# Another written order and another choice of engines for a recurrent attention with a Fourier mix and an FFN

## The chip, the core and the metric

The kernel runs on one core of a Trainium2 chip. The metric is the device time of one execution in microseconds (us). The core has TensorE (PE, matrix products; its weight loads are listed as PEld), VectorE (DVE), ScalarE (ACT), GpSimd (POOL) and SyncE (SP, which issues transfers). Each engine works through its own queue in order; an instruction that waits holds up all that stand behind it on that engine.

## What is computed

Four batches of 768 rows; eight heads of 64 make 512 columns. First a linear recurrence with one decay for each head, then the real part of a two-dimensional Fourier transform added to its input, a normalisation of each row, and an FFN of width 2048 with a residual:

```python
for t in range(S):
    state = gamma[None, :, None, None] * state + einsum('bhd,bhe->bhde', k[:, :, t], v[:, :, t])
    y[:, :, t] = scale * einsum('bhd,bhde->bhe', q[:, :, t], state)
...
x = y.transpose(0, 2, 1, 3).reshape(B, S, H * D)
u = x + real(fft(fft(x, axis=1), axis=2))
un = (u - mean(u)) / sqrt(var(u) + 1e-06)
out = u + relu(un @ w_ch1) @ w_ch2
```

## The kernel before

The recurrence is done in chunks of 128 rows. Heads go in pairs, so there are four pairs (the last number of a piece's name, 0 to 3) and six chunks. For each pair the queries, keys and values are loaded (`lq`, `lk`, `lv`, by SP), cast to 16 bit (`q`, `k`, `v` in batch 0, `cq`, `ck`, `cv` in the later ones) and transposed on PE through PSUM (`tq`, `tk`), from where an engine copies them (`eq`, `ek`). In batch 0 the keys are transposed back (`kb`, copy `eb`). PE forms the products of queries and keys (`am`, later `a`, L574 and L694), DVE masks them (`ae`, L583; later `m`, L705), PE forms the states (`kv`), DVE runs them through the decay (`sc`, a scan, L607; later `s1` to `s4`, L731), PE forms the output from state and masked product (`yx`, `yi`, later `y`), and an engine scales its rows (`x`). The Fourier transform over the rows folds the rows first (`fs`, `fl`, `fh`, `fd`, `fe` on DVE, L785 to L811), multiplies with cosine and sine tables (`s1..`, then copies `g`, `gr`), and does the columns by a second product (`s2`), whose halves are combined into u by DVE (`u0`, `u1`, after a copy `q0`, `q1`) and the input added (`ux`, by POOL or DVE). `g0a`, `g0b`, `g0c` are a small edge column. Statistics of the rows (`bn` on DVE, `rt` on ACT, `rc`, `nb`) give the normalised rows (`un`), which are transposed (`ut`, `te`). In the FFN `h` is the first product with the weights and `r` its relu; the second one adds its 2048 terms in the order of a fast matrix product: sums of halves of relu results (`hs`, on DVE, L1300) go into products (`m1a` to `m7b`, L1329) and sums of those into u (`w`, L1374).

Batch 0 is also the start. While its first loads run, the tables of cosines and sines are made on the chip: steps 0 to 4 of `ta` (product, L403), `tn` (rounded copy), `tb` (product, L406) and `ab`, `co`, `si` on ACT. Batches 1, 2 and 3 follow, and the FFN of one batch is mixed with the attention of the next.

What sets the order: every piece of work is a function in a dictionary, and the table ORDER lists all their names. `play` (L1591) calls them one after another, and `pin` (L232) ties the instructions of each engine into that order. So ORDER is an order for all five queues at once, and only the place of a piece among the pieces of its own engine counts, beside its data. Buffers are taken in this order as well: products of PE go to five PSUM buffers of one group, to two of another and, after the start, to three of a third, and a product waits until the buffer's last reader is done.

A second table, ENGINES, names the engine of each piece that more than one can do: A, D or P for ACT, DVE, POOL. The helpers `copied` (L260) and `scaled` (L265) take that letter and issue the copy or the scaling there; a relu, an addition of x and a few more read it in their own pieces.

The piece `f512` is `filler(512)` (L257, L258): a product of 128x128 with 128x512 zeros into a PSUM buffer that nobody reads. It is given 16 times in ORDER; eight more are issued before ORDER begins.

Loads of batch 1 wait for two things: a load of weights (`w22`) and the matmul `h13` of the first FFN half of batch 0. Loads of later batches wait for a product of the batch before.

Of the kernel before, what the change touches and what calls it, by code (L numbers as in the profile page):

```python
# [18 lines left out]
P = 128  # L19
B, H, S, D = 4, 8, 768, 64  # L20
# [22 lines left out]
h12:A qn4:A h13:A xu2:D h03:A un2:A h11:A h01:A te2:A xl4:P xu4:P xu3:P xl0:D un3:A xu0:D h10:A
h20:D un4:A h21:A qn5:D xl5:P 1ck1_0:P te3:A h22:A 1cq_0:D 1ck0_0:D 1ek_0:D 1eq0_0:A 1eq1_0:A
xu5:P 1cv_0:P 1s0_0:A un5:A 1cq_1:A te4:D 1ck0_2:A 1ck0_1:P 1ck1_1:P mp7:P 1eq1_1:A 1eq0_1:A
1cv_1:P 1ek_1:A 1x1_0:A mp3:P 1x0_0:A h23:A 1cv_2:P 1ck1_2:A 1s0_1:D te5:A 1cq_3:P 1cq_2:A
1ck0_3:P 1s0_2:D 1cv_3:P 1ek_2:A mp4:P 1eq1_2:A 1ck1_3:P 1eq0_2:A 0r1_12:A 1eq1_3:A 1eq0_3:A
1x1_1:A 1x0_1:A 1s0_3:A 0r1_5:A 1ek_3:A 0r1_7:A 0r1_8:A 1x0_2:A 1x1_2:A 2cv_1:A 2cq1_1:A
# [47 lines left out]
0h1_12 2cq1_1 1kv1_2 1m2_2 1a0_3 0r1_6 2lk2 0r1_12 mp4 1s3_2 0h1_11 0r1_11 1s4_2 1m0_3 1a2_3 1m2_3
# [1532 lines left out]
```

## Time and profile before

| | |
|---|---|
| median of three runs | 235.96 us (235.61 to 236.78) |
| profiled execution | 236.86 us |
| its span, first to last instruction | 234.9 us |
| busy: PE, DVE, ACT, POOL | 228.9, 203.4, 144.3, 91.3 us |
| granted clock | 1.0 |
| bytes: read, written | 27.26, 6.29 MB |

A row of the profile's timeline has the start in us, the duration, the engine, the line of the kernel, the operation, the tiles as out<-in, the shapes and a count of like instructions that were put together; in brackets stands the idle time of the engine before it and what ended it. A row of grouped instructions has instead the busy time in us, the mean duration of one in ns, and the idle time ahead of the group with what ended it. Instructions of one engine that follow directly on each other overlap a little in the records.

### The profile page before, as it was taken

How to read it: one execution, taken by the hardware profiler on the slowest of the kernel's cores; microseconds unless marked ns; L12 is line 12 of the kernel's file. 1: busy time of each engine (PE TensorE's matmuls, PEld its weight loads, DVE VectorE, ACT ScalarE, POOL GpSimd, SP SyncE). 2: the span in 40 equal slices, each digit the busy share in tenths (PEclk: the TensorE clock that was granted, in tenths of full speed). 3: DMA queues.
4: the chain of work that ended last, by engine and by line, in shares of the span. 5: the costliest groups of instructions: out<-in, count | busy, mean ns of one | idle time of the engine just before them, and what ended most of it. 6: DMA issues, size and time to landing. Idle time of an engine off the chain costs nothing.

```text
span 234.9 us, 6332 instructions
## 1 busy us (share of the span) xinstructions
PE 228.9 (97%) x2471; PEld 187.1 (80%) x2471; DVE 203.4 (87%) x527; ACT 144.3 (61%) x303; POOL 91.3 (39%) x144
## 2 busy tenths in 40 slices
PE   7999999999999999999999999999999999999994
PEld 2566888856776855889999989888898988888884
DVE  6599989966899999999999999999988698875494
ACT  7599786688998856671976493565644615241220
POOL 4789133452440378226315707404007161330302
PEclk9999999999999999999999999999999999999999
DMA  7999997999999999999969956632700224130034
GB/s 199 311 290 178 207 166 116 257 228 247 220 213 201 211 209 176 198 195 182 237 161 202 201 129 126 156 77 81 237 3 4 45 89 114 22 47 0 4 125 143
DMA packets 94253, 36.45 MB, mean 155 GB/s; under 512 B 83600, under 2 KB 91408, under 8 KB 94224
## 3 DMA queue, kind: packets, MB, share of 16 engines
q1 hardware_dynamic: 89856, 31.79, 63.9%
q0 software_dynamic: 4224, 4.19, 11.5%
q8 instruction: 19, 0.31, 0.6%
q14 instruction: 10, 0.08, 0.1%
q10 hardware_dynamic: 144, 0.07, 0.1%
HBM read 27.26 MB, written 6.29 MB: 143 GB/s over the span
## 4 chain that ended last, share of the span: by engine, by line
PE 73%; ACT 1%; DVE 0%; issue 0%
PE psh L1267 27%; PE psc L1329 24%; PE psc L1223 6%; PE psh L1183 4%; PE wkA L694 3%; PE ps L840 3%; PE pq L1024 2%; PE wkY L753 2%; PE wkY L744 1%; PE wkK L717 1%; ACT qTz L262 1%; PE tq L669 1%; PE psh L1205 0%; PE pst L1167 0%; PE ps L974 0%; ACT x L267 0%
## 5 line engine op out<-in xcount | busy, mean ns | idle before, releaser
L1267 PE MATMUL psh<-unT,w 128*128 128x256 f16 x576 | 67.7, 273 | 0.0
L1267 PEld LDWEIGHTS <-w 128*128 128x128 f16 x576 | 55.8, 98 | 6.6 <-DVE u L1374 0.2
L1276 ACT ACTIVATE ht<-psh 128x512 f16<-128x512 f32 x65 | 37.4, 596 | 30.5 <-PE psh L1267 22.7
L1329 PEld LDWEIGHTS <-ht 128*128 128x128 f16 x360 | 34.1, 98 | 4.2 <-DVE ht L1300 0.3
L1329 PE MATMUL psc<-w,ht 128*128 128x256 f16 x192 | 26.2, 272 | 0.0
L705 DVE TENSOR_TENSOR atm<-wkA,maskp 128x512 f16<-128x512 f32 x36 | 23.9, 682 | 1.5 <-PE wkA L694 1.5
L1060 POOL TENSOR_TENSOR u<-u,x 128x256 f32<-128x256 f32 x31 | 19.7, 654 | 14.2 <-DVE u L1050 7.9
L1223 PE MATMUL psc<-w,ht 128*128 128x512 f16 x96 | 23.3, 379 | 0.0
L1374 DVE TENSOR_TENSOR u<-psc,u 128x256 f32<-128x256 f32 x42 | 16.7, 416 | 6.6 <-PE psc L1329 5.8
L1374 POOL TENSOR_TENSOR u<-u,cd 128x512 f32<-128x512 f32 (+1 forms) x8 | 8.9, 1119 | 27.9 <-DVE cd L1374 27.9
L267 ACT ACTIVATE x<-wkY,gexp 128x384 f16<-128x384 f32 x29 | 16.1, 583 | 5.6 <-PE wkY L753 4.1
L731 DVE SCALAR_TENSOR_TENSOR s<-s,gk,wkK 128x128 f16<-128x128 f16 x48 | 16.1, 341 | 2.2 <-ACT s L262 1.5
L1118 DVE BATCH_NORM_STATS2 bst<-u 128x6 f32<-128x512 f32 x24 | 16.3, 681 | 0.2
L263 POOL COPY g16r<-g 128x384 f16<-128x384 f16 x6 | 3.4, 579 | 31.5 <-ACT g L262 19.0
L1223 PEld LDWEIGHTS <-ht 128*128 128x128 f16 x96 | 8.7, 98 | 7.7
L262 ACT COPY qn<-pq 128x127 f32<-128x127 f32 (+2 forms) x31 | 7.9, 299 | 11.0 <-PE pq L1024 5.1
L1374 POOL TENSOR_TENSOR u<-u,ws 128x256 f32<-128x256 f32 (+1 forms) x6 | 5.7, 978 | 20.5 <-DVE ws L1374 20.5
L1399 ACT ACTIVATE un<-u,stats 128x512 f16<-128x512 f32 x12 | 9.5, 812 | 5.8 <-DVE stats L1392 5.8
L694 PE MATMUL wkA<-qTz,kT 128*128 128x256 f16 x72 | 12.4, 272 | 0.3 <-ACT unT L262 0.2
L268 POOL TENSOR_SCALAR kd<-k,gexp 128x384 f16<-128x384 f32 x15 | 9.4, 629 | 6.8 <-DMA k<-in_k_dram 4.8
L1183 PE MATMUL psh<-unT,w 128*128 128x384 f16 x64 | 11.9, 326 | 0.0
L1205 PE MATMUL psh<-unT,w 128*128 128x128 f16 x192 | 11.7, 219 | 0.0
(238 smaller groups left out, 508.5 us busy)
## 6 DMA issues: line engine op xcount, KB each, us to landing
q<-in_q_dram SPq DMA_DIRECT2D x16, 384.0 KB, 6.2
k<-in_k_dram SPq DMA_DIRECT2D x16, 384.0 KB, 5.6
v<-in_v_dram SPq DMA_DIRECT2D x16, 384.0 KB, 6.3
w<-in_moe_w_ch_dram POOLq DMA_DIRECT2D x8, 512.0 KB, 7.8
out_dram<-u SPq DMA_DIRECT2D x6, 512.0 KB, 3.4
out_dram<-u SPq DMA_DIRECT2D x6, 256.0 KB, 3.9
out_dram<-o SPq DMA_DIRECT2D x2, 512.0 KB, 3.2
out_dram<-o SPq DMA_DIRECT2D x3, 128.0 KB, 1.8
```

Source lines behind the costliest of these rows:

```text
L267: return nc.scalar.activation(out, in_, AF.Copy, bias=0.0, scale=scale)
L694: mm = nc.tensor.matmul(wk[:, c2], st["kT"][:, c, :], st["qT"][:, :, c, :], start=True, stop=True)
L705: nc.vector.tensor_tensor(out=st["atm"][:, 2 * part:2 * part + 2], in0=st["wk", part], in1=maskp[:, PAIR_ORDER[i]].unsqueeze(1).to_broadca ...
L731: nc.vector.scalar_tensor_tensor(out=s16[:, c], in0=s16[:, c - 1], scalar=gk2[:, hp:hp + 1], in1=st["kv", c // 3][:, c % 3], op0=ALU.mult, ...
L1060: (nc.vector if on.get(f"{b}ux{n}_{kb}", "P") == "D" else nc.gpsimd).tensor_tensor(out=u[:, lo:hi], in0=u[:, lo:hi], in1=x[:, 1, 257:1:-1] ...
L1118: nc.vector.bn_stats(bst, lb[b]["u"][:, kb, :])
L1183: nc.tensor.matmul(psh, w116[:, cb, fb * P:(fb + 1) * P], lb[b]["unT"][:, cb, rt * 384:(rt + 1) * 384], start=(cb == 0), stop=(cb == 3))
L1223: nc.tensor.matmul(lb[b]["psc", rb], ht16[:, fb, rb % 3 * P:rb % 3 * P + P], w216[:, fb, :], start=(fb == 0), stop=(fb == NFB - 1))
L1267: nc.tensor.matmul(psh[:, t], w116[:, cb, fb * P:(fb + 1) * P], lb[b]["unT"][:, cb, p * 256:(p + 1) * 256], start=(cb == 0), stop=(cb == 3))
L1276: nc.scalar.activation(dst, psh, AF.Relu, bias=0.0, scale=1.0)
L1329: nc.tensor.matmul(o if c1 - c0 == 256 else o[:, c0:c1], lh(f), r, start=first and f == 0, stop=last and f == 7, skip_group_check=True)
L1374: (nc.vector if e == "D" else nc.gpsimd).tensor_tensor(out=o, in0=x, in1=y, op=ALU.add)
```

## The change

Only the two tables change; no function does.

ORDER is written anew from its first name to its last. It has the same pieces, except that `f512` stands in it ten times, not sixteen (1444 names for 1450). Of the pieces named in ENGINES or left to a default some hundred go to another engine; the count of entries goes from 239 to 242 for ACT, 68 to 63 for DVE, 104 to 106 for POOL.

The start of both tables, and the pieces of batch 1 and of the late stretch that the prediction speaks of:

```diff
 ENGINES = """
-q0:A q1:P q2:A q3:P k00:D k10:P k20:P k30:A v00:P v10:P v20:P v30:P v31:P eq0:D eq1:D eq2:A
-eq3:A ek00:A ek10:A ek20:A ek30:A x00:A x01:D x10:A x11:D x20:A x21:A x30:A x31:A tn0:D tn1:A
-tn2:D tn3:D tn4:A gk0:P gk1:A gk2:P gk3:A gc00a:D gc01a:D gc01b:D gc10a:A gc11a:A gc11b:A
...
+q0:A q1:P q2:D q3:D k00:D k10:P k20:P k30:A v00:P v10:P v20:P v30:P v31:A eq0:A eq1:A eq2:A
+eq3:A ek00:D ek10:A ek20:A ek30:A x00:D x01:A x10:A x11:A x20:A x21:A x30:A x31:A tn0:A tn1:D
+tn2:A tn3:A tn4:D gk0:A gk1:P gk2:P gk3:P gc00a:D gc01a:A gc01b:A gc10a:A gc11a:D gc11b:A
...
 ORDER = """
-lq0 nid0 lk0 par gk3 f512 q0 lv0 qtz10 lq1 ta0 v00 ta1 tn1 f512 f512 f512 f512 tb1 si1 k00 tk0 qz0
-q1 mp2 lk1 lv1 lq2 qtz00 lk2 ab1 tq0 lq3 tn0 gk2 eq0 tb0 ta2 tn2 f512 ek00 am01 ab0 ae010 nid1 kb0
-k10 co1 tb2 si2 hid5 ab2 co2 ae011 tq1 am00 ae001 si0 f512 f512 eb0 ta3 tk1 ek10 lk3 f512 tn3 eq1
-tb3 lv2 ab3 v01 kv0 ae000 yi01 kb1 gk0 v11 sc0 si3 q2 mp6 f512 v10 f512 k20 gk1 nsp yi00 co0 eb1
-am11 ae110 ae111 am10 ae101 ae100 tk2 ek20 tq2 yx0 eq2 x01 kv1 q3 f512 x00 f512 f512 w10 w11 sc1
-am21 ae210 ae211 am20 mp3 ae201 yi10 k30 ae200 kb2 eb2 yi11 yx1 x11 f512 x10 fs0a fs0b tk3 ta4 tq3
-v20 ek30 v21 kv2 sc2 tn4 tb4 w12 kb3 eq3 am30 yi20 ae301 mp7 ae300 ab4 am31 hid ae311 si4 eb3 yi21
-yx2 ae310 stx01 lv3 v30 v31 kv3 s1s10 w13 w20 sc3 x20 x21 flb yi31 yi30 co4 fla fd1 yx3 f512 s1s00
-x30 fd0 s1m1 x31 fha fhb co3 cdh0 xn0 g0a s1m0 xm0 gc00a s1s01 gc01a gc10a xmb xn1 s1s11 gc11b
...
-uu3 qn5 ul5 xl5 xu3 h11 pad11 ut2 te2 h13 1lq0 1lk0 h10 1lq1 xu0 bn0 1lk1 h22 bn1 bn3 xu4 1lv0 h20
-h21 0rt0 bn4 0p1_0 uu5 0p2_0 un3 h12 1cq_1 0p3_0 xu5 0p0_2 1cq_0 1tq0 1tq1 1ck1_0 1ck1_1 1ck0_0
...
+par lq0 qz0 nid1 ta0 f512 mp2 gk2 f512 f512 q0 tq0 lk0 mp4 ta1 nid0 tn0 tb0 k00 tk0 f512 tn1 gk0
+eq0 si0 qtz00 tb1 hid5 ab0 si1 ta3 tn3 lk1 lq1 k10 tk1 ek10 ek00 am00 f512 kb0 q1 tq1 mp5 ae000
+lv0 ae001 ab1 co1 v00 kb1 eb1 eb0 eq1 tb3 lk2 ta2 v01 lq2 k20 tn2 gk3 gk1 am01 ae010 am10 ae101
+ae100 co0 ab3 si3 tb2 kv0 ae011 am11 si2 f512 ab2 tk2 ek20 co2 yi01 yi00 nsp q2 tq2 kb2 ae110 co3
+sc0 yx0 eq2 mp7 eb2 x01 lv1 v10 v11 lk3 ae111 k30 mp1 f512 kv1 w10 x00 am20 w11 am21 sc1 yi10 yi11
+yx1 tk3 x11 ta4 f512 f512 ae211 lq3 q3 ae201 lv2 v20 v21 x10 tq3 ek30 kb3 eq3 am31 w12 ae200 ae210
+yi20 eb3 tn4 tb4 ab4 fs0b fs0a co4 ae311 g0a kv2 si4 sc2 lv3 v31 am30 f512 g0b v30 yi21 yx2 x20
+kv3 x21 w13 ae300 xn1 s1s10 ae310 yi30 cdh0 ae301 yi31 sc3 yx3 x30 fla w20 x31 xn0 s1s00 flb fd0
+hid s1m0 fd1 s1m1 xm0 gc10a qe1 fha fhb s1s11 gc00a s1s01 gc11b stx01 stx3 stg00 xmb gc01a gc01b
...
+xl2 s24 un2 0p0_0 un1 qn3 ut1 te1 mp3 h01 w23 uu3 h13 1lq1 1lq0 h11 ul3 xl3 qn5 h02 h10 ul5 xl5
+uu5 1lk0 qn4 0p1_0 0p2_0 xu3 bn3 ul4 xu0 ut2 te2 h12 uu4 xu4 bn2 qtz01 h22 xl4 bn1 pad11 h20 1cq_1
+h21 1lk1 bn0 0rt0 mp6 un3 0p0_1 xu5 ut3 te3 0p1_1 1cq_0 1tq0 1ck0_0 1eq0_0 1ck0_1 bn5 1eq1_0 bn4
...
```

In batch 1 the casts of queries 1cq_0 (before on DVE), 1cq_1 and 1cq_2 (before on ACT) go to POOL. Between the half sums 2hs1_1 and 2hs1_2 of batch 2, 3gr01 goes from DVE to POOL, 3q0_0, 3q0_2, 3q1_2 and 3q0_3 from DVE to ACT, and 2r2_1, 3g00, 3q1_0 (before on ACT), 3ux1_0, 3ux0_1 and 3ux0_3 (before on POOL) to DVE; the pieces 3u1_2 and 3u0_3, always on DVE, are written ahead of 2hs1_2.

More of the change, by code (lines that the diff above doesn't have):

```diff
@@ L43 @@
[L43 to L48, printed above, removed]
@@ new lines @@
+tn2:A tn3:A tn4:D gk0:A gk1:P gk2:P gk3:P gc00a:D gc01a:A gc01b:A gc10a:A gc11a:D gc11b:A
+ste0:A ste1:A xn0:A xn1:P cdh0:A cdh1:D nsp:P hid5:A fs0a:D fs0b:D fla:D flb:D fha:D fhb:D
+fd0:D fd1:D gr0:D gr1:P gr2:P gr3:A nid0:D nid1:P hid:P v01:P eb0:D v11:P eb1:D v21:P eb2:D
+eb3:A mp2:P mp6:P mp3:A mp7:P qn2:A qn1:D un1:A h00:A h03:D xl2:P qn0:A qn3:A xu2:P te1:A xl3:D
+h01:A h02:A un2:D mp0:D xl0:P qn4:A xl4:P qn5:D xl5:D xu3:P h11:A te2:A h13:A h10:A xu0:P h22:A
+xu4:D h20:A h21:A un3:D h12:A 1cq_1:P xu5:P 1cq_0:P 1ck1_0:D 1ck1_1:P 1ck0_0:P un4:D 1ek_0:D
@@ new lines @@
+hid s1m0 fd1 s1m1 xm0 gc10a qe1 fha fhb s1s11 gc00a s1s01 gc11b stx01 stx3 stg00 xmb gc01a gc01b
+stx4 stg01 cdh1 stg10 gc11a stg11 close gr3 xm2 g0c mu2 s22 gr0 qn2 ul2 w21 stx2 w22 px1 xm1 mu1
+ste1 ste0 s21 xe qn1 uu1 ul1 gr2 gr1 qz1 s23 uu2 s20 qn0 xu2 ul0 h03 h00 uu0 qtz11 xl0 s25 half
+xl2 s24 un2 0p0_0 un1 qn3 ut1 te1 mp3 h01 w23 uu3 h13 1lq1 1lq0 h11 ul3 xl3 qn5 h02 h10 ul5 xl5
+uu5 1lk0 qn4 0p1_0 0p2_0 xu3 bn3 ul4 xu0 ut2 te2 h12 uu4 xu4 bn2 qtz01 h22 xl4 bn1 pad11 h20 1cq_1
+h21 1lk1 bn0 0rt0 mp6 un3 0p0_1 xu5 ut3 te3 0p1_1 1cq_0 1tq0 1ck0_0 1eq0_0 1ck0_1 bn5 1eq1_0 bn4
@@ L162 @@
+3m30_2 3w30_2 3sb0 3m31_2 3w31_2 3sb1
 """
```

200 lines of the change are left out of this document (98 added, 102 removed).

## The prediction

> **What bounds the kernel now.** I read the page's shares and slices first, then the engines' busy time by stretch, then TensorE's (PE's) order of time, then that of VectorE (DVE), which stands next.
>
> ```profile
> PE 228.9 (97%) x2471; PEld 187.1 (80%) x2471; DVE 203.4 (87%) x527; ACT 144.3 (61%) x303; POOL 91.3 (39%) x144
> PEclk9999999999999999999999999999999999999999
> 0.00:10.00 10.00, 8.75 (x30) 3.47 (x30) 5.45 (x34) 6.58 (x13) 4.98 (x18) 1.00 0.89 240
> 10.00:20.00 10.00, 9.87 (x149) 6.32 (x150) 9.68 (x19) 9.02 (x20) 9.06 (x14) 1.00 1.17 262
> 20.00:30.00 10.00, 9.65 (x146) 7.66 (x145) 9.28 (x21) 8.49 (x18) 5.17 (x12) 1.00 1.24 207
> 50.00:60.00 10.00, 9.39 (x93) 6.49 (x94) 7.01 (x16) 9.01 (x15) 3.15 (x6) 1.00 1.16 239
> 80.00:100.00 20.00, 20.00 (x169) 13.22 (x167) 19.12 (x45) 12.86 (x33) 12.73 (x21) 1.00 1.26 202
> 140.00:160.00 20.00, 20.00 (x212) 17.78 (x210) 19.56 (x50) 10.40 (x23) 7.88 (x10) 1.00 0.51 110
> ```
>
> In the stretches the columns are length, busy time of PE, weight loads, DVE, ACT, POOL, granted clock, DMA share, GB/s. PE is full in the long stretches, so a gain can only come from work taken off PE or from gaps in the first 60 us. DVE has 0.4 to 0.9 us in 20 to spare: it is the bound that stands directly behind PE. Full PE is not all useful, though:
>
> ```profile
> 1.25 4.02 PE L258 MATMUL wps<-ht 128*128 128x512 f16 x9 [1.25 <-DVE ht L312]
> 7.96 1.48 PE L531 MATMUL tq<-ident,q16z 128*128 128x128 f16 x12
> 9.24 0.53 PE L406 MATMUL tab<-tmp,nid 128*128 128x386 f16 x1
> 10.93 0.51 PE L555 MATMUL tq<-ident,kT 128*128 128x128 f16 x6
> 11.27 0.33 PE L406 MATMUL tab<-tmp,nid 128*128 128x386 f16 x1
> 14.84 0.59 PE L258 MATMUL wps<-ht 128*128 128x512 f16 x2
> 15.27 0.34 PE L620 MATMUL wkY<-v,atm 128*128 128x64 f16 x6
> 50.21 0.51 PE L669 MATMUL tq<-ident,q16z 128*128 128x128 f16 x6 [0.28 <-ACT q16z L267]
> 56.37 0.27 PE L717 MATMUL wkK<-v,kd 128*128 128x128 f16 x2 [0.23 <-ACT kT L262]
> 57.03 0.38 PE L694 MATMUL wkA<-qTz,kT 128*128 128x256 f16 x2 [0.17 <-ACT unT L262]
> ```
>
> Two fillers (L258, a product that nobody reads) start at 14.84 and the next matmul at 15.27: 0.43/2 = 0.215 us each. Twelve transposes from 7.96 to 9.24 take 1.28/12 = 107 ns each, six of the same size from 10.93 to 11.27 take 57: PE runs at half rate until about 10 us, although the granted clock reads full throughout. The last three rows are the gaps that the profile names after the start: 0.28 + 0.23 + 0.17 = 0.68 us, all behind ACT.
>
> **The fillers and the start.** Sixteen fillers stand in the written order, ten remain: 6 x 0.215 = 1.3 us of PE work removed. If fillers only occupy PE while it would wait for DVE, this is worth nothing unless the chain that PE waits for is shorter too. That chain in the rows of DVE:
>
> ```profile
> 9.48 0.96 DVE L268 TENSOR_SCALAR qTz<-tq 128x768 f16<-128x768 f16 x1 [2.71 <-PE tq L531]
> 11.11 1.70 DVE L583 SCALAR_TENSOR_TENSOR atm<-wkA,maskf 128x384 f16<-128x384 f32 x3 [0.20 <-PE wkA L574]
> 12.72 0.55 DVE L268 TENSOR_SCALAR kd<-tq 128x768 f16<-128x768 f16 x1
> 13.19 0.42 DVE L268 TENSOR_SCALAR tmp<-tab 128x257 f16<-128x257 f32 x1
> 14.85 0.81 DVE L607 TENSOR_TENSOR_SCAN s<-gk,wkK 128x320 f16<-128x320 f32 x1
> 15.58 0.53 DVE L268 TENSOR_SCALAR kd<-tq 128x768 f16<-128x768 f16 x1
> 22.11 1.03 DVE L785 TENSOR_TENSOR xab<-x 128x774 f16<-128x774 f16 x2 [0.53 <-ACT kT L267]
> 23.79 1.93 DVE L583 SCALAR_TENSOR_TENSOR atm<-wkA,maskf 128x384 f16<-128x384 f32 x4
> 25.66 0.82 DVE L607 TENSOR_TENSOR_SCAN s<-gk,wkK 128x320 f16<-128x320 f32 x1
> ```
>
> DVE stands idle 2.71 us before the first copy of transposed queries (eq0) and is then full until the fourth scan ends at 26.48. The change gives eq0 and eq1 to ACT, whose row for the same copy is 0.81 us against 0.96, and transposes the queries alone, after three fillers, not together with a table product and the keys. I put the first mask product at 10.3 to 10.8 us: 0.3 to 0.8 earlier. DVE's work from there to the fourth scan becomes 16 masks at 1.93/4 = 0.48, four scans at 15.58 - 14.85 = 0.73, three kd at 13.19 - 12.72 = 0.47, two casts of queries (q2, q3; nearest row the cast of keys, 0.56), two folds (1.03 the pair), one row scaling (0.6), one table step (0.5), and g0a, which moves ahead of the scan (0.9): 7.7 + 2.9 + 1.4 + 1.1 + 1.0 + 0.6 + 0.5 + 0.9 = 16.1 us. Before it was 26.48 - 11.11 = 15.37 with 0.73 of idle in it, and g0a came after: 15.5 to compare. So 0.6 us more work, 0.3 to 0.8 earlier, 0.73 of idle that may or may not vanish: from -0.9 us to +0.3. With PE's own 1.3 as the bound on the good side and, should the first mask come no earlier and a wait of the size of the 0.53 row be new, +0.7 on the bad side. I take -1.0, near the good end, because the idle ahead of eq0 is by far the largest one here and the change goes straight at it.
>
> **Gaps at 50 to 57 us.** They come from queries of batch 1 cast late:
>
> ```profile
> 49.31 0.84 ACT L267 ACTIVATE q16z<-q 128x768 f16<-128x768 f32 x1 [0.72 <-DMA q<-in_q_dram]
> 51.09 0.56 DVE L263 COPY kT<-tq 128x768 f16<-128x768 f16 x1 [1.68 <-PE tq L669]
> 53.88 1.29 DVE L705 TENSOR_TENSOR atm<-wkA,maskp 128x512 f16<-128x512 f32 x2 [0.52 <-PE wkA L694]
> 56.52 0.35 DVE L731 SCALAR_TENSOR_TENSOR s<-s,gk,wkK 128x128 f16<-128x128 f16 x1 [1.14 <-ACT s L262]
> ```
>
> The cast waits 0.72 us for its load, the second transposes wait for the cast, and DVE loses 1.68 + 0.52 + 1.14 = 3.3 us behind them. The loads of batch 1 are released by the matmul h13 of the first FFN half. h13 stands some 2 us earlier in the new order, the first query load (1lq1) goes ahead of 1lq0, and 1cq_0, 1cq_1, 1cq_2 go to POOL, 39% busy. POOL's cast of that size has a row of 0.83 us, as long as ACT's 0.84, so what counts is only that ACT need not do it between its copies. I take the 0.7 us of named gaps as closed; the good bound is 1.45, the sum of the excess between starts of neighbours at these places, the other nothing.
>
> **The body.** The engines' sums hardly change (counted by the rows' durations, DVE 229.6 to 229.7 us, ACT 159.0 both, POOL 85.3 to 85.8), so engine swaps are worth something only by place. From the fourth scan to the half sum 1hs1_0, DVE's work by the tables goes from 161 pieces and 81.7 us to 162 and 82.2: +0.56. I take half, +0.3, with 0 and +0.6 as ends, for the 3.3 us of idle just named can absorb it. Moved loads (lk0 and lk1 ahead of lv0) change places in SP's queue and not their number; what is late for it is v of batch 0, first read by the scan's product behind the first masks. Sum: -1.0 - 0.7 + 0.3 = -1.4 us.
>
> The profiled execution took 236.86 us (a span of 234.9 and 1.96 around it), 0.9 above the median of 235.96. 236.86 - 1.4 = 235.5, or on the median **234.6 us**. Ends: -1.3 - 1.45 + 0 = -2.75 (233.2) and +0.7 + 0 + 0.6 = +1.3 (237.3).
>
> **Rivals.**
>
> *Slower: DVE takes over late.* Between the half sums 2hs1_1 and 2hs1_2:
>
> ```profile
> 172.53 0.69 DVE L1300 TENSOR_TENSOR ht<-s1h,ht 128x1024 f16<-128x1024 f16 x1
> 173.88 0.42 DVE L1374 TENSOR_TENSOR u<-psc,u 128x256 f32<-128x256 f32 x1 [0.37 <-PE psc L1329]
> 177.62 1.28 DVE L1374 TENSOR_TENSOR u<-psc,u 128x256 f32<-128x256 f32 x3 [0.69 <-PE psc L1329]
> 183.68 0.16 DVE L1147 RECIPROCAL stats<-stats 128x1 f32<-128x1 f32 x1 [0.78 <-ACT stats L1141]
> 185.72 0.29 DVE L263 COPY qn<-pq 128x128 f32<-128x128 f32 x1 [0.64 <-PE pq L1024]
> 187.64 0.69 DVE L1300 TENSOR_TENSOR ht<-s1h,ht 128x1024 f16<-128x1024 f16 x1
> 188.39 1.05 PE L1329 MATMUL psc<-gk,ht 128*128 128x256 f16 x8
> L1060 DVE TENSOR_TENSOR u<-u,x 128x256 f32<-128x256 f32 x5 | 2.7, 564 | 0.0
> L1278 DVE TENSOR_SCALAR ht<-psh 128x512 f16<-128x512 f32 x7 | 4.8, 686 | 1.8 <-PE psh L1267 1.8
> ```
>
> The second sum ends at 188.33, its matmul 2m6a_2 starts at 188.39: 0.06 us of slack. Ahead of it five small DVE pieces go (3gr01, 3q0_0, 3q0_2, 3q1_2, 3q0_3, some 0.27 each: 1.36) and eight come: three adds with x (0.5 to 0.56), a relu of 0.69, a copy of 0.6, a small one of 0.28, and two u pieces (0.47): 4.0 in all. That is +2.66, less 0.25 for three more neighbours that overlap by 0.08 each (12.72 + 0.55 against 13.19 above): +2.4, while PE's work in the same piece of order stays (14.8 to 14.6). DVE's idle there is 0.37 + 0.69 + 0.78 + 0.64 = 2.5. If all of it is filled, the loss is nothing; the waits for ACT's root (0.78) and for the query product (0.64) belong to pieces that are ordered the same, and if these two stay, DVE is 1.4 us late. It decides from the point where more than 0.1 us of the idle stays, and it takes the gain too, since DVE in the full stretches from 80 to 160 us runs no earlier than now. 235.96 + 1.4 = 237.4 us; with all idle kept 238.4. For it: slacks of this size and DVE above 95%. Against it: ACT is at 61% and gives results early.
>
> *No gain.* The removed fillers stood in waits for DVE, the start is set by DVE's sum (+0.6 more work, 0.3 to 0.8 earlier), the gaps close in part and the body takes that back: -1.0 falls to 0, -0.7 + 0.3 remain, 235.6 us.
>
> *The half rate lasts longer.* With fewer fillers PE may reach 57 ns later than at 10 us. Half a window of the observed kind, say the six transposes and six products up to 10.93 again at half rate, costs 12 x 50 ns = 0.6, and two such places 1.2: 234.6 + 1.2 = 235.8. Against it: eight fillers ahead of the order are left alone (the 4.02 us row). [...]
>
> *More.* DVE's idle by 60 us all goes: 233.2.
>
> **How the numbers follow.** Two runs of this kernel can be told apart from about 0.5%, 1.2 us. Chances: the forecast 0.37, more 0.05, so faster 0.42; no gain 0.17, half rate 0.05, so the same 0.22; DVE late 0.36, so slower 0.36. The range goes from 233.0, just below the sum's good end, to 238.4, the price of the rival with its idle kept; where the sum falls short of 1.2 us it has become the case without gain, so the forecast's own range is 233.2 to 234.8.
>
> **What would show it.** Right: the first mask product (L583) by 10.8 us, the fourth scan ending by 26.3 with g0a ahead of it, no row with a wait above 0.2 us on PE from 49 to 58 us. Wrong: idle time on PE behind L1300, L705 or L731 of DVE after 60 us, above all at the matmul behind 2hs1_2; or small waits on PE spread over the body, which no single row above foretells.

## The result, and the profile after

| | before | after |
|---|---|---|
| median (17 runs each) | 235.69 us | 237.46 us |
| lowest to highest | 234.82 to 237.12 | 236.85 to 238.9 |
| ratio to before, 95% interval | | 1.0078 (1.0056 to 1.0101) |
| profiled execution, its span | 236.86, 234.9 us | 238.25, 236.1 us |

The changed kernel is 0.8% slower. The time lies in the range given, but on the side opposite to the forecast of 234.6 us. It lies close to what the slower rival gave (237.4), and that is chance: what that rival described did not happen.

The page of the changed kernel, shares and granted clock in 40 slices, and the busy time by stretch (columns as in the prediction; the granted clock is the third number from the end):

```profile
PE 225.9 (96%) x2465; PEld 186.6 (79%) x2465; DVE 206.6 (88%) x522; ACT 144.3 (61%) x306; POOL 93.1 (39%) x146
PEclk9989999999999999999999999999999999999999
0.00:10.00 10.00, 6.45 (x34) 2.69 (x35) 6.12 (x33) 7.13 (x15) 4.69 (x19) 1.00 0.79 227
10.00:20.00 10.00, 8.69 (x125) 6.31 (x121) 8.24 (x15) 7.85 (x16) 8.20 (x14) 0.83 1.03 246
50.00:60.00 10.00, 10.00 (x104) 6.93 (x102) 8.82 (x22) 8.30 (x13) 5.05 (x8) 1.00 1.16 236
200.00:220.00 20.00, 19.50 (x179) 17.16 (x178) 13.47 (x36) 4.96 (x11) 3.32 (x4) 1.00 0.21 43
```

PE is busy 3.0 us less than in the profile of before (228.9 us), and the kernel is longer: PE now waits. That is not 3.0 us of work removed: a second profile of before, the run before_again below, has PE busy 226.1 us, as PE left its half rate earlier in it (near 4.5 us and not near 10). The gaps between 50 and 60 us are gone (10.00 of 10 us, before 9.39). In their place 3.55 us are missing in the first ten, the clock falls below full speed in the next ten (0.83 in the row), and 0.5 us are missing between 200 and 220. The waits, in the order of time of PE:

```profile
4.65 0.82 PE L257 MATMUL wps<-ht 128*128 128x512 f16 x3
5.39 0.51 PE L530 MATMUL tq<-ident,q16z 128*128 128x128 f16 x6
7.76 0.27 PE L402 MATMUL tab<-trow,tcolf 2*128 2x257 f16 x1 [0.61 <-ACT tmp L421]
9.71 0.51 PE L530 MATMUL tq<-ident,q16z 128*128 128x128 f16 x6 [1.69 <-POOL q16z L267]
11.84 0.85 PE L554 MATMUL tq<-ident,kT 128*128 128x128 f16 x6
17.01 0.51 PE L530 MATMUL tq<-ident,q16z 128*128 128x128 f16 x6 [0.77 <-DVE q16z L267]
18.19 0.53 PE L629 MATMUL wkY<-s,qTz 64*128 64x64 f16 x10 [0.34 <-DVE s L606]
213.47 1.92 PE L1266 MATMUL psh<-unT,w 128*128 128x256 f16 x16 [0.50 <-DMA unT<-un]
231.61 1.05 PE L1328 MATMUL psc<-w,hsum 128*128 128x128 f16 x16 [0.27 <-DVE o L1373]
```

The transposes of the second pair's keys (tk1, at 9.71) stand ahead of the first query-key product in the new order and wait 1.69 us for a cast that waits for its load. The size of this wait differs between executions: it is 0.37 and 0.56 us in the profiles of late_before and ww22_first and absent in those of s_after and us5_early, four kernels with the same start. Some 2 us behind it, six back-transposes take 0.85 us as a group where six of them take 0.51 at full rate: PE runs at half rate. The clock by stretch says when:

```profile
8.00:10.60 2.60, 0.91 (x14) 0.62 (x14) 0.00 (x0) 0.79 (x3) 1.53 (x2) 1.00 0.97 245
10.60:14.10 3.50, 3.50 (x34) 2.61 (x32) 2.35 (x5) 2.99 (x6) 3.13 (x7) 0.52 1.09 295
14.10:16.00 1.90, 1.90 (x34) 1.33 (x35) 1.90 (x5) 1.69 (x6) 0.62 (x1) 0.98 1.12 339
```

To follow the loss through the kernel I take, at a given matmul, the time at its end less the usual durations of all useful products up to it (fillers not counted), from the trace of each kernel. It grows only where PE waits, runs at half rate or does something nobody needs. "At 25 us" stands for the matmul at which 25 us of useful products are done, about 41 us into the kernel; 54, 190 and 196 lie at about 71, 207 and 213 us.

| profiled execution of | at 25 | at 54 | at 190 | at 196 | last matmul ends | span |
|---|---|---|---|---|---|---|
| before | 16.4 | 17.8 | 18.1 | 18.1 | 231.7 | 234.9 |
| after | 17.5 | 17.6 | 18.0 | 18.7 | 232.7 | 236.1 |

So the changed kernel loses 1.1 us in the start, wins 1.3 between 41 and 71 us, holds level through the whole body, loses 0.7 at 213 us and 0.6 in its last rows (0.4 up to the last matmul, the rest behind it). Within the body the profile names one wait of PE from 60 to 190 us, 0.30 us for a sum on DVE:

```profile
129.24 0.60 PE L1328 MATMUL psc<-w,ht 128*128 128x256 f16 x4 [0.30 <-DVE u L1373]
```

### The profile page after: what moved, and what is told of

Same layout as the page of the kernel before. It is cut to its first block, busy times and chain, and to the rows that moved or that the text cites. A ratio compares the mean times of both kernels' runs of the same rounds, so it can differ in the third digit from the quotient of the medians.

```text
span 236.1 us, 6285 instructions
## 1 busy us (share of the span) xinstructions
PE 225.9 (96%) x2465; PEld 186.6 (79%) x2465; DVE 206.6 (88%) x522; ACT 144.3 (61%) x306; POOL 93.1 (39%) x146
## 4 chain that ended last, share of the span: by engine, by line
PE 84%; DVE 5%; DMA 5%; ACT 3%; issue 1%; SPq 0%; POOL 0%; DVEq 0%
PE psh L1266 25%; PE psc L1328 20%; PE psc L1222 9%; PE psh L1204 5%; PE psh L1182 4%; PE wkA L693 3%; DMA k<-in_k_dram 3%; PE ps L839 3%; PE pq L1023 2%; PE wkY L752 2%; DMA unT<-un 2%; PE wkY L743 2%; PE wkK L716 1%; PE tq L668 1%; PE pq L1073 1%; DVE u L1373 1%
## 5 line engine op out<-in xcount | busy, mean ns | idle before, releaser
L1275 ACT ACTIVATE ht<-psh 128x512 f16<-128x512 f32 x64 | 37.0, 596 | 23.5 <-PE psh L1266 16.2
L266 ACT ACTIVATE x<-wkY,gexp 128x384 f16<-128x384 f32 x30 | 16.4, 583 | 5.2 <-PE wkY L752 4.0
L1373 POOL TENSOR_TENSOR u<-u,cd 128x512 f32<-128x512 f32 (+1 forms) x8 | 7.9, 998 | 23.7 <-DVE cd L1373 23.7
L1117 DVE BATCH_NORM_STATS2 bst<-u 128x6 f32<-128x512 f32 x24 | 16.4, 681 | 0.8 <-POOL u L1059 0.7
L261 ACT COPY qn<-pq 128x127 f32<-128x127 f32 (+2 forms) x37 | 9.3, 291 | 10.6 <-DVE u L1049 3.0
L267 POOL TENSOR_SCALAR kd<-k,gexp 128x384 f16<-128x384 f32 x18 | 11.2, 627 | 6.6 <-DMA k<-in_k_dram 6.6
L267 POOL TENSOR_SCALAR q16z<-q 128x384 f16<-128x384 f32 (+1 forms) x14 | 9.6, 689 | 10.4 <-DMA q<-in_q_dram 9.2
L1373 POOL TENSOR_TENSOR u<-u,ws 128x256 f32<-128x256 f32 (+1 forms) x6 | 5.6, 946 | 19.7 <-DVE ws L1373 17.2
```

The costliest lines, as they stand in the source:

```text
L266: return nc.scalar.activation(out, in_, AF.Copy, bias=0.0, scale=scale)
L267: return (nc.gpsimd if e == "P" else nc.vector).tensor_scalar(out=out, in0=in_, scalar1=scale, scalar2=1.0, op0=ALU.mult, op1=ALU.mult)
L1117: nc.vector.bn_stats(bst, lb[b]["u"][:, kb, :])
L1275: nc.scalar.activation(dst, psh, AF.Relu, bias=0.0, scale=1.0)
L1373: (nc.vector if e == "D" else nc.gpsimd).tensor_tensor(out=o, in0=x, in1=y, op=ALU.add)
```

## The experiments

All are timed against the unchanged kernel before, in the same session; ratios are the ones to compare, since that kernel's own median moved from 235.1 to 235.9 us between sessions.

**Where is it lost?** The two orders reach the name close (about 31 us) with nearly the same pieces behind them, and again 2m5b_2 (190 us) and 3r2_7 (226 us). There one order can be continued by the other, with the engines of each.

```diff
 s_before:    ORDER, ENGINES of before up to close, then after
 s_after:     after up to close, then before
 late_before: after up to 2m5b_2, then before
 tail_before: after up to 3r2_7, then before
```

> The old kernel's order and engines up to the end of the start (the name close, at about 31 us), the changed kernel's from there on. Theory (the loss is made in the start): matmul for matmul the changed kernel stands 1.05 us behind the old one at 31 us, so this one should come to 237.46 - 1.05 = 236.4 us or a ratio of 1.003 to the old kernel, with the gaps at 50 to 57 us gone as in the changed kernel. Rival (the loss is made by the vector queue between 80 and 190 us, as my prediction's slower case had it): the start is given back later and this one stays at 237.2 to 237.5.

Measured: 1.0023 (0.9991 to 1.0056), as the first theory had it. The seam cost it 0.56 us of a wait on PE at 33.9 us which neither parent has, so the figure is an upper one.

> The changed kernel's start up to close, the old kernel's order and engines from there on. Theory (the start costs 1.05 us, nothing takes it up later): 235.69 + 1.05 = 236.7 us, ratio 1.0045. Rival (vector queue of the body decides): the same as the old kernel, 235.7 within 0.3, as the old body has idle time at 50 to 57 us to take the lag up.

Measured: 1.0014 (0.9983 to 1.0045), 236.37 us, between the two. Its profile shows the same order of start as the changed kernel's, but no half rate after PE has reached its full rate (the moment that the expectations call the release), and a loss of 16.3 us at 25, no more than the 16.4 of the old kernel's first profile. Together the two come to 0.0037 of the 0.0078. Each is uncertain by 0.003, so what is missing may be noise or something that needs both halves; that stays open.

> The changed kernel up to about 190 us (the name 2m5b_2), the old kernel's order and engines from there to the end. Theory (0.8 us are lost behind a transposed row block at 213 us and in what follows, and 0.4 at the end of the last sums and stores): 237.46 - 1.2 = 236.3 us. Rival (loss in the body ahead of 190 us): 237.3 to 237.5, no change.

Measured: 0.9989 (0.9963 to 1.0015). The late stretch gives back all of the 0.8% and more than the 1.2 us expected. Its profile is of an execution with 6.8 us at half rate, that of the changed kernel of one with 3.4, so their spans (234.7 and 236.1 us) understate the gain. The vector queue between 80 and 190 us, which the rival blamed, is in this kernel as in the changed one.

> The changed kernel up to about 226 us (3r2_7), the old kernel's order for the last pieces. Theory (0.6 us of the late loss are made there, POOL's two additions standing ahead of the last rows' additions on DVE): 237.46 - 0.6 = 236.9 us. If the end only shows what was lost at 213 us: 237.4.

Measured: 1.0043 (1.0013 to 1.0073), a gain of 0.35% over the changed kernel for the last rows alone. The difference of the two ratios is uncertain by 0.004, so this gain isn't clear of the noise by its times.

**The half rate and the fillers.**

```diff
 fill6 (after)
-si1 ta3 tn3 ... nsp q2 tq2 ... sc0 yx0
+si1 f512 f512 ta3 tn3 ... nsp q2 f512 f512 f512 tq2 ... sc0 f512 yx0
 strip6 (before)
-f512 tn3 eq1 ... q2 mp6 f512 v10 f512 k20 ... q3 f512 x00 f512 f512 w10
+tn3 eq1 ... q2 mp6 v10 k20 ... q3 x00 w10
```

> The changed kernel with six fillers put back, where PE waits in its start: two ahead of the table product ta3 (wait 0.61 us), three ahead of the transposes tq2 (0.77 to 0.94), one ahead of the state product yx0 (0.34). Theory (the waits let the clock of PE fall to half, 10.7 to 14.1 us in one execution and 17.5 to 24.4 in two others, which costs the start some 1.1 us in most executions): no stretch of granted clock below 1.0, the idle-free work of PE at 30 us as in the old kernel (16.3 to 16.4 us of it not useful, against 17.4), and 237.46 - 0.9 = 236.6 us. Rival (the fillers only stand in waits, the half rate is hidden behind DVE): 237.3 to 237.6.

> The old kernel with six fillers less: the ones at 13.30, 14.84 (two) and 17.91 us (three). Theory (fillers keep the clock): waits of 0.2 to 0.65 us appear in their places, the clock falls to half for 3.4 or 6.8 us in most executions, and the time is 235.8 + 0.8 = 236.6 us. Rival one (six fillers are 1.3 us of PE work that something waits for): 234.9. Rival two (they stand in waits and nothing else): 235.8 within 0.3.

Measured: 1.0039 (1.0014 to 1.0063) with the six put back, a gain of the size expected (0.0039, uncertain by 0.0033), and no granted clock below 1.0 in the span of its profile. The old kernel without six: 0.999 (0.9962 to 1.0017). Its rival two is right: there the six stand in waits and keep nothing; its twelve executions have a granted clock of 1.0 throughout. In the old kernel, then, six fillers less cost and win nothing that these runs can tell. Of the six profiles with the changed kernel's own start (the first 31 us unaltered), three show the clock at half, one at 10.6 to 14.1 us, two at about 17.5 to 24.4; this is one of those, with the late part of before:

```profile
14.00:17.50 3.50, 2.16 (x36) 1.58 (x34) 3.50 (x6) 2.12 (x5) 3.36 (x6) 1.00 1.26 275
17.50:24.30 6.80, 6.39 (x68) 4.45 (x67) 5.17 (x12) 4.56 (x8) 4.63 (x7) 0.50 1.11 182
```

The stretch ahead of the fall has PE busy 2.16 of 3.5 us. That share alone doesn't decide. In the profile of q2_act, below, PE is busy 1.68 of 3.41 us and keeps its full rate in the stretch behind:

```profile
13.82:17.23 3.41, 1.68 (x32) 1.45 (x30) 1.80 (x4) 3.19 (x6) 2.85 (x5) 1.00 1.24 293
17.23:20.65 3.42, 3.21 (x67) 2.38 (x64) 3.09 (x6) 2.21 (x4) 3.35 (x5) 1.00 0.91 142
```

How often a fall comes can be counted, as the mean granted clock of each execution is on record: 3.4 us at half rate in 236 make it 0.993, 6.8 us make it 0.986.

| kernel | executions | clock 0.993 or less | their times | median of the others |
|---|---|---|---|---|
| after | 17 | 4 | 238.23 to 238.9 us | 237.39 us |
| late_before | 12 | 2 | 236.78, 236.96 | 235.62 |
| fill6 | 12 | 1 | 237.18 | 236.50 |
| q2_act | 6 | 3 | 238.38 to 239.58 | 237.02 |
| best | 6 | 6 | 236.35 to 238.24 | |

So the fall costs an execution of the changed kernel 1.2 us and comes in about a quarter of them. The other 13 have a median of 237.39 us, still 0.7% above before: the half rate isn't what makes the changed kernel slower. By the executions without it fill6 stands at 1.005 and the changed kernel at 1.007, so a part of what the six fillers win is not the clock; the wait at 213 us isn't in the profile of fill6 either. Fillers don't exclude a fall: the kernel best has two of them and fell in all six of its executions.

**The late stretch.**

```diff
 us5_early (after)
-3u0_4 3rc5 3h1_5 ... 3us4 3ut4 3us5 ... 3ut5 3h2_5
+3u0_4 3rc5 3us5 3ut5 3h1_5 ... 3us4 3ut4 ... 3h2_5
 ww22_first (after)
-3hs21_2 3m6a_2 3m6b_2 3w6_2 3sb_0 3sb_1 3hs30_2 3ww12_2 3ww22_2
+3hs21_2 3hs30_2 3m6a_2 3m6b_2 3w6_2 3sb_0 3sb_1 3ww12_2 3ww22_2
```

> The changed kernel with the normalised rows 3us5 and their transposing transfer 3ut5 moved from behind 3us4, 3ut4 to right behind the reciprocal 3rc5, where DVE stands idle. Theory (PE waits at 213 us for that transfer alone, 0.63 us between its matmuls): no wait there, 237.46 - 0.65 = 236.8 us. Rival (the other block, 3ut4, lands no earlier, or the half sums behind it are late anyway): 237.3 or more.

Measured: 1.0046 (1.002 to 1.0072), and no wait at that place. In six of eight profiles of kernels with the changed kernel's order there, it costs 0.7 to 0.9 us; in s_before and fill6 it isn't there. So the order makes the wait likely and not certain, and what else decides is not known.

> The changed kernel with the sum of relu halves 3hs30_2 ahead of 3w6_2 in the last rows, as in the old one, so that DVE's addition 3ww22_2 starts together with POOL's 3ww12_2 and not 0.1 us behind it. Theory (DVE's addition takes 0.95 us in place of 0.42 because POOL's, of the same kind, began first; the next sums and the wait of 0.27 us on PE follow from it): 3ww22_2 back at some 0.42 us, the wait gone, 237.46 - 0.5 = 237.0 us. Rival (POOL's addition slows DVE's in either order): 0.95 us again and 237.3 or more.

Measured: 1.005 (1.0024 to 1.0077). The ratios of us5_early and ww22_first each lie 0.003 below that of the changed kernel, and these differences are uncertain by 0.0035: that either edit gains something rests on the waits that are gone from its profile (at 213 us, and the 0.27 us at 231 us), not on the times alone. The pair of additions, first the changed kernel, then this one:

```profile
229.49 0.95 DVE L1373 TENSOR_TENSOR u<-u,ws 128x256 f32<-128x256 f32 x1
229.38 1.64 POOL L1373 TENSOR_TENSOR u<-u,ws 128x256 f32<-128x256 f32 x2 [6.00 <-DVE ws L1373]
```

```profile
228.25 0.43 DVE L1371 TENSOR_TENSOR u<-u,ws 128x256 f32<-128x256 f32 x1
228.36 1.59 POOL L1371 TENSOR_TENSOR u<-u,ws 128x256 f32<-128x256 f32 x2 [6.19 <-DVE ws L1371]
```

DVE starts 0.11 us behind POOL and takes 0.95 us, or 0.11 us ahead of it and takes 0.43.

**The gaps at 50 to 57 us.**

```diff
 cq_pool (before)
-1cq_0:D 1cq_1:A 1cq_2:A
+1cq_0:P 1cq_1:P 1cq_2:P
 h13_early (before)
-h01 w23 h02 ... h13 1lq0 1lk0 h10 1lq1
+h01 w23 h13 1lq1 1lq0 h02 ... 1lk0 h10
 tq1_later (before)
-1cq_0 1tq0 1tq1 1ck1_0 ... bn5 0p1_2 1ek_0
+1cq_0 1tq0 1ck1_0 ... bn5 0p1_2 1tq1 1ek_0
```

> The old kernel with the casts 1cq_0, 1cq_1 and 1cq_2 on POOL as in the changed one (1cq_0 from DVE, the others from ACT), order unchanged. Between 30 and 60 us the old kernel loses 1.4 us of PE time, the changed one 0.1. Theory (the engine of the casts makes it): most of it comes back, 235.8 - 0.9 = 234.9 us. Rival (the loads of batch 1 come earlier behind the earlier h13, and the engine matters little): the wait for the load stays and the time is 235.8 within 0.3.

Measured: 1.0066 (1.0039 to 1.0093), slower: two transposes at 49.5 us wait 1.39 us for POOL, which casts both after the load.

> The old kernel with the first-half product h13 and the two query loads 1lq1, 1lq0 moved ahead of h02, some 3 us earlier on PE. Theory of my prediction (the gaps at 50 to 57 us are late loads, released by h13): the wait of ACT for the queries is gone, PE's lost time between 30 and 60 us falls from 1.4 to 0.4 us or less, 0.4% faster than the old kernel. Rival (the transfers fill the DMA engines and land no earlier): lost time above 1.0 us, no change within 0.2%.

Measured: 1.0055 (1.0029 to 1.0082), slower, for a reason of its own: h13 waits 1.36 us at 39 us for a copy on DVE. The loss from 48 to 71 us falls to 0.6 and ACT no longer waits for the load, so the loads were part of it, but with the new wait ahead of them this doesn't prove it.

> The old kernel with the transposes 1tq1 moved behind the second-half product 0p1_2, 2 us later on PE, about where the changed kernel has them; loads and engines as before. Theory (the gaps went because the transposes stand later in PE's order, not because data come earlier): the gap ahead of 1tq1 (0.28 us named, 0.45 between starts) is gone and nothing takes its place, PE's lost time between 30 and 60 us falls from 1.4 to 0.9 us, 0.2% faster. Rival (the copies of 1tq1 come late for the products): the same sum of gaps, at other places.

Measured: 0.9994 (0.9966 to 1.0022). The gap ahead of 1tq1 is gone, the loss between 41 and 71 us is 0.9 against 1.4 us, and the time can't be told from no change. What closed these gaps in the changed kernel is not settled: neither the engine nor the load alone, and the place only in part.

**Late stretch and fillers together.**

> The changed kernel with the six fillers back in the waits of its start and with the old kernel's order and engines from about 190 us (2m5b_2) on. Theory (the two gains shown apart, 0.9 us of the clock and 1.8 of the late stretch, add up): 1.0078 - 0.0039 - 0.0075 = 0.9964 of the old kernel, so some 0.8 us faster than it. Rival (the two share a cause, or the old kernel's early release of the clock in unprofiled executions makes up for it): 1.000 within 0.002.

Measured: 1.0009 (0.9984 to 1.0033): the gains don't add up, and something in the start is still longer than before. Three kernels look for it, a fourth joins them.

```diff
 k1_later (after)
-lk1 lq1 k10 tk1 ek10 ek00 am00 f512 kb0 q1 tq1
+lk1 lq1 k10 ek00 am00 f512 kb0 q1 tk1 ek10 tq1
 q2_act (after)
-q2:D
+q2:A
 nsp_later (after)
-yi01 yi00 nsp q2 ... v10 v11 lk3
+yi01 yi00 q2 ... v10 v11 nsp lk3
```

> The changed kernel with tk1 and its copy ek10 moved behind the first query-key product am00 and the back-transposes kb0. Theory (a): the product waits for nothing but eq0 and ek00 and starts at 8 to 8.5 us, not 10.2, the first mask follows it, and the chain of DVE to the fourth scan ends 0.6 to 1.5 us earlier; 1.0078 falls to some 1.004. Rival (b or c alone): DVE waits later for the second pair's keys or queries instead, scan four ends within 0.3 us of where it ended (about 26.8 in an execution without the half rate), ratio 1.007 or more.

Measured: 1.0085 (1.0057 to 1.0114). The first product starts earlier (at 9.12 us, in the changed kernel at 10.16) and the rest waits for the second pair's keys anyway: the loss at 25 is 16.2 us, though its q2 took 0.55 us, as it began 0.06 us ahead of POOL's copy and not behind it. My theory (a) falls.

> The changed kernel with one letter changed: the cast q2 on ACT (0.84 us there), as in the old one. Theory (b): DVE is rid of 1.3 to 1.5 us, PE's wait ahead of tq2 (0.77 to 0.95 us) is gone, scan four ends 0.8 us or more earlier, ratio 1.0078 - 0.004 = 1.004. Rival (a or c): ACT, which then has the cast, gives the copies eq1 or eq2 later by as much; ratio 1.007 or more.

Measured: 1.0115 (1.0078 to 1.0151), slower. Three of its six executions fell to half rate; the other three, at 1.008, are as the changed kernel. ACT casts at 15.8 us, behind the table pieces and copies that the new order puts ahead of it, and the wait of PE ahead of tq2 grows to 1.73 us. Theory (b) in the form "give it back to ACT" falls too: in the new order ACT has no room there.

> The changed kernel with POOL's copy nsp (1158 elements, 1.16 us) moved behind its casts v10 and v11, so that it no longer runs beside DVE's cast q2. Theory (b by overlap): q2 takes 0.55 to 0.6 us on DVE and the wait ahead of tq2 falls below 0.2 us, ratio about 1.005. Rival (a cast of queries is slow on DVE whatever POOL does): 1.3 us or more again, and no change.

Measured: q2 takes 0.55 us and the wait ahead of tq2 is gone, as expected of the overlap; the loss at 25 is 15.5 us against 16.2. The time, 1.0067 (1.0039 to 1.0096), hardly shows it: the wait for the transposed rows at 213 us is 0.9 in this profile. Three meetings of the cast with POOL, DVE's rows first. In us5_early, with the changed start, POOL's copy nsp begins 0.09 us ahead of the cast:

```profile
13.93 1.49 DVE L265 TENSOR_SCALAR q16z<-q 128x768 f16<-128x768 f32 x1
15.34 0.54 DVE L580 SCALAR_TENSOR_TENSOR atm<-wkA,maskf 128x384 f16<-128x384 f32 x1
13.84 1.16 POOL L265 TENSOR_SCALAR ht<-ssp 128x1158 f16<-128x1158 f16 x1 [0.50 <-ACT ssp L422]
```

In k1_later the same copy begins 0.06 us behind the cast. The cast takes 0.55 us, and POOL's copy pays, with 1.51 in place of 1.16:

```profile
14.87 0.55 DVE L265 TENSOR_SCALAR q16z<-q 128x768 f16<-128x768 f32 x1
14.93 1.51 POOL L265 TENSOR_SCALAR ht<-ssp 128x1158 f16<-128x1158 f16 x1 [1.56 <-ACT ssp L422]
```

In nsp_later the cast meets POOL's scaling of v instead, which is recorded as beginning 0.08 us ahead of it. Here POOL pays too (two scalings take 1.56 us, in us5_early 1.14):

```profile
14.40 0.55 DVE L265 TENSOR_SCALAR q16z<-q 128x768 f16<-128x768 f32 x1
14.32 1.56 POOL L265 TENSOR_SCALAR v<-v,gexp 128x384 f16<-128x384 f32 x2 [0.80 <-DMA v<-in_v_dram]
```

> The changed kernel with tk1 later, q2 on ACT, two fillers ahead of ta3 and the old kernel's order and engines from about 190 us on. If (a), (b) and the late stretch account for the loss, the start's work that is not useful is below 15.5 us at 30 us (16.2 without the half rate, 17.4 with it, in the changed kernel), and the time is 0.995 of the old kernel, about 234.5 us. If not, 1.000 as with the fillers and the late part alone.

Measured: 1.0094 (1.0064 to 1.0124), a miss: it carries q2 on ACT, and all its six executions fell to half rate, as three of the six of q2_act did.

**The same kernel twice, and the last combination.** nsp_late is nsp_later with two fillers ahead of ta3, one ahead of yx0, and the old kernel's order from 190 us on.

> The old kernel once more, nothing changed. Theory (the moment of the release decides 1.5 us of the start and is drawn anew in each execution): times spread over some 2.5 us in two groups, ratio 1.000 within 0.003, and the profile shows either the release near 10 us with 16.4 us of PE time that is not useful at 30 us, or one near 4 us with 14.9. Rival (the release belongs to the kernel): near 10 us again, and a spread without groups.

Measured: 1.0022 (0.9996 to 1.0048), which is also how far two sets of runs of one kernel can lie apart. Its times spread over 2.5 us, as expected, but no two groups stand apart in twelve executions. Its profile has a span of 233.1 us against 234.9, nearly all of it from the start (1.5 us at 25):

```profile
4.84 0.50 PE L403 MATMUL tab<-trow,tcolf 2*128 2x386 f16 x2
6.31 0.84 PE L531 MATMUL tq<-ident,q16z 128*128 128x128 f16 x12
8.20 0.34 PE L574 MATMUL wkA<-qTz,kT 64*128 64x128 f16 x6
7.19 0.96 DVE L268 TENSOR_SCALAR qTz<-tq 128x768 f16<-128x768 f16 x1
8.64 1.02 DVE L583 SCALAR_TENSOR_TENSOR atm<-wkA,maskf 128x384 f16<-128x384 f32 x2
24.16 0.82 DVE L607 TENSOR_TENSOR_SCAN s<-gk,wkK 128x320 f16<-128x320 f32 x1
```

The twelve transposes take 0.84 us as a group (1.48 in the first profile), the copy eq0 begins at 7.19 with no idle time ahead of it (9.48, and 2.71), the fourth scan ends at 24.98 (26.48). Five other kernels here begin with the old order. In the profiles of four (s_before, strip6, h13_early, tq1_later) the twelve transposes take 1.48 or 1.49 us, in that of cq_pool 0.83. So the late full rate is the commoner one with the old start, five profiles of seven.

> The changed kernel with POOL's nsp behind v10 and v11, two fillers ahead of ta3 and one ahead of yx0, and the old kernel's order and engines from about 190 us on. Theory (cast, clock and late part account for the loss): 15.3 to 15.5 us not useful at 30 us, no stall at 213 us, ratio 0.998, that is 1.0009 of the fillers with the late part less 0.003 for the cast. Rival (the cast's gain is taken back by the body, as it seemed to be with nsp_later alone): 1.001 or more.

Measured: 235.14 us against 235.69, 0.9969 (0.9941 to 0.9997): without the slow cast, with fillers in three of the waits and with the old late stretch the changed kernel is no slower than the kernel before, and faster by about as much as two sets of runs of one kernel were seen to differ.

| profiled execution of | at 25 | at 54 | at 190 | at 196 | last matmul ends | span |
|---|---|---|---|---|---|---|
| before, once more | 14.9 | 16.1 | 16.3 | 16.3 | 229.9 | 233.1 |
| s_after (no half rate) | 16.3 | 17.0 | 17.2 | 17.2 | 230.8 | 234.0 |
| us5_early (no half rate) | 16.2 | 16.3 | 16.7 | 16.7 | 230.7 | 234.1 |
| late_before (half rate) | 17.4 | 17.5 | 18.0 | 18.0 | 231.5 | 234.7 |
| nsp_later | 15.5 | 16.0 | 16.5 | 17.4 | 231.4 | 234.8 |
| nsp_late | 15.5 | 15.9 | 16.7 | 16.7 | 230.2 | 233.4 |

## Why the prediction was wrong, point by point

**The start, -1.0 us.** This is the first step that failed. Measured by itself, in s_after, the new start is worth +0.3 us, between -0.4 and +1.1. The -1.0 was also more than the working gave: the sum of DVE's chain ended at -0.9 at best.

*First*, the 2.71 us of idle time ahead of eq0, "by far the largest one here", was taken as gain. It isn't in every execution: it goes with a full rate of PE that comes near 10 us, in five of seven profiles with the old start; in the second profile of before the rate came at some 4.5 us, the idle time was nothing, and the loss at 25 was 14.9 in place of 16.4 us. The profiled 236.86 us lay above the median of 235.96, which I noted and did not ask the reason of. The new order did remove the late rate: in all thirteen profiles that begin with it or a variant of it the full rate came before 7.3 us. But the time did not follow, as other waits came in: without a later fall the new start has still lost 16.2 to 16.3 us at 25 (s_after, us5_early), about as much as the old one with its late rate (16.4) and 1.3 us more than with its early one. Why the rate comes early in the new order is not shown.

*Second*, the two casts of queries given to DVE were priced at 0.56 us each, by the row of a cast of that size. q2 took 1.28 us in the changed kernel and 1.48 or 1.49 in six others (s_after, late_before, fill6, fill6_late, us5_early, ww22_first), q3 0.55 to 1.26. My row was of a moment in which POOL did nothing: it stands at 5.40 us, and POOL is busy 0.00 us from 4 to 7. POOL's copy nsp began 0.29 us ahead of q2 in the changed kernel and 0.09 in late_before and us5_early. The 0.7 us between nsp_later (15.5) and the others (16.2) is the part of that error that q2 makes in the start, by these profiles; in the time it is not shown alone (1.0067 against 1.0078).

*Third*, the work that PE waits for: I had the first mask product at 10.3 to 10.8 and it stood at 10.61. That is luck, as the wait for the second keys holds it there; in us5_early, with the same start and without that wait, it stands at 9.75. The fourth scan ended at 27.90 and not by 26.3. In us5_early it ends at 26.76, so that 1.1 us of it are the half rate of this execution and the rest is in every one.

**The fillers.** That 1.3 us of PE work could be worth nothing was said, and strip6 shows it for the old kernel: the same time without them. That the bound of 1.3 was taken as nearly reached was a mistake.

**The rival of the half rate**, with 5 in 100, had PE reach its full rate later. That did not happen; PE lost the rate again after stretches with waits, for 3.4 or 6.8 us. The price of 0.6 us for each of two places was near, 1.2 us in an execution with a fall, but 13 of 17 executions had no fall of such a length. That fillers bring the full rate sooner was a guess of mine that no run shows: with the same fillers it came near 10 us and near 4.5 in the two profiles of before.

**The gaps at 50 to 57 us, -0.7 us** (bound -1.45). Right in sign and between the bounds: -1.3 us against the first profile of before, -1.1 against the second. The reason given, earlier loads and POOL's casts, isn't shown. POOL's casts alone made the old kernel slower.

**The body, +0.3 us.** From 54 to 190 us of useful work the old kernel loses 0.3 us and the changed one 0.4. The sign and the ends are right; of the +0.3 taken 0.1 came, and the wait of 0.30 us for DVE at 129 us is the kind of thing that it priced.

**The slower rival, DVE late at 2hs1_2.** Wrong. That sum and its matmul in the changed kernel:

```profile
186.27 0.69 DVE L1299 TENSOR_TENSOR s1h<-ht 128x1024 f16<-128x1024 f16 x1 [0.70 <-ACT ht L1275]
187.80 0.69 DVE L1299 TENSOR_TENSOR ht<-s1h,ht 128x1024 f16<-128x1024 f16 x1
188.55 1.05 PE L1328 MATMUL psc<-gk,ht 128*128 128x256 f16 x8
```

The slack is 0.06 us as before, and DVE even idles 0.70 us shortly ahead, waiting for ACT. Between the two half sums DVE is busy 13.39 us where it was 11.25, and PE is busy throughout in both kernels, first before, then after:

```profile
173.22:187.64 14.42, 14.42 (x144) 13.03 (x143) 11.25 (x32) 8.00 (x19) 5.50 (x8) 1.00 0.09 20
172.95:187.80 14.85, 14.85 (x154) 13.21 (x151) 13.39 (x35) 7.19 (x18) 5.93 (x8) 1.00 0.11 32
```

DVE's added 2.1 us (2.4 were forecast) made PE wait nowhere here, the case that I had priced at nothing: the waits for ACT's root and for the query product fell from 0.78 and 0.64 us to 0.15 and none.

**What was not in the sum at all** is the late stretch, the second step that failed. The order behind 190 us was written anew too, and I gave it no term. It holds the larger part: late_before takes the ratio from 1.0078 to 0.9989, clear of the noise, and by the tables the changed kernel loses 1.3 us more behind 190 than before (span less the figure at 190: 218.1 us, against 216.8 in both profiles of before). The two places found are the transfer 3ut5 behind 3ut4 (us5_early, 1.0046) and POOL's addition ahead of DVE's (ww22_first, 1.005); each by its profile rather than by its time, and the first not in every kernel with that order. It could have been suspected from the tables: the transposing transfer stood second instead of first, and by the changed kernel's profile issuing one takes 1.20 or 1.22 us.

What stays open: what closed the gaps at 50 to 57 us, 0.6 us of the new start (15.5 against 14.9 us at 25), and why the start and the rest, taken apart, cost only half of what they cost together.

## What to carry to other kernels

A single profile is one draw. Where its own time lies some way off the median, as here by 0.4%, find the stretch that differs before pricing a gain there; a second profile of the unchanged kernel would have shown that the largest idle time of this one is absent in some executions. An order that is rewritten whole has to be walked to its last row, since the last rows have no work behind which a wait can hide. And a duration taken from a row may not hold beside other work: the same cast on DVE took 0.55 us here or 1.49, so look at what POOL does at the same moment.

## What the runs showed of the hardware

PE's rate. Until some moment between 4 and 10 us, PE runs at half rate (107 ns for a transpose of 128x128, 57 after it), and the moment differs between executions of one kernel: near 10 us and near 4.5 in the two profiles of before. The granted clock in the profile's rows reads 1.00 through this first phase and only shows a later fall. That fall came after stretches with waits in them (PE busy 0.91 of 2.6 us, or 2.16 of 3.5) and lasted 3.4 us (the changed kernel) or 6.8 (late_before); in the longer case PE was busy 6.39 of 6.80 us at half rate. A stretch with PE busy 1.68 of 3.41 us was followed by full rate in q2_act, so the share of busy time doesn't decide by itself. What does decide, and what sets the moment of the first full rate, these runs don't show.

DVE beside POOL. An addition took 0.95 us on DVE where POOL's began 0.11 us earlier (the changed kernel), 0.43 where DVE began 0.11 us earlier (ww22_first); a cast took 1.49 us where POOL's copy had begun 0.09 us ahead (us5_early), 0.55 where it began 0.06 us ahead of that copy (k1_later), and then the copy took 1.51 us in place of 1.16. In us5_early POOL's copy ends at 15.00 us and the cast 0.42 us behind it; in k1_later the cast ends at 15.42 us and the copy 1.02 us behind it. In rows without such a delay the cast takes 0.55 us and the copy 1.16. What causes the delay these runs don't show. In nsp_later POOL's scaling of v is recorded as beginning 0.08 us ahead of the cast and is the one that takes longer (1.56 us for two, 1.14 in us5_early), so a tenth of a microsecond in the recorded starts doesn't by itself tell who pays.
